# A long convolution and two expert layers: PSUM laid out by stage, the imaginary product in a pair of banks, both folds on VectorE, and the first products at another pace

## The chip, the cores and the metric

The kernel runs on one core of a Trainium2 chip. The core has five engines that run side by side and wait for each other through semaphores: TensorE (PE: matmuls, and PEld: their weight loads), VectorE (DVE), ScalarE (ACT), GpSimd (POOL) and SyncE (SP), whose queue issues nearly all DMA transfers. SBUF is the working memory. PSUM is the small memory that matmuls write; here it is used as 8 banks of 512 fp32 words for each of 128 partitions. [...]

The metric is the device time of one execution in microseconds (us).

## The reference

```python
def _attn_ref(x, v, pos_emb, w1, w2):                    # S = 12480, D = 128
    h_filt = (np.maximum(pos_emb @ w1, 0.0) @ w2) * np.exp(-0.01 * np.arange(S))[:, None]
    u = x * v
    Uf = np.fft.rfft(u, n=2 * S, axis=1)
    Hf = np.fft.rfft(h_filt, n=2 * S, axis=0)
    y = np.fft.irfft(Uf * Hf[None, :, :], n=2 * S, axis=1)[:, :S, :]
    return x * y

def reference(...):
    x = attn_out                                         # 12480 tokens of 128 channels
    x = (np.maximum(x @ w_in, 0.0) ** 2) @ w_out         # 2048 hidden units
    h = x @ w_in2
    return (np.maximum(h, 0.0) + alpha * np.minimum(h, 0.0)) @ w_out2
```

## The kernel before

The convolution is computed in the frequency domain, on a grid of 110 x 229 points, with small dense transform matrices instead of an FFT. Its work is cut into these parts:

- The filter: `z_stage` and `ar_stage` compute the filter's values and their first transform; `r_stage` does the second in 28 steps of two frequencies and spills the result to DRAM, 14 pieces.
- The signal, in two halves of 64 channels: `u_stage(h)` has 16 groups of four channels (k = 16h to 16h + 15) and runs in 17 steps. A step holds `u_mm_a` of one group and `u_mm_b` of the group before. `u_mm_a` is 16 matmuls (line 267) into two banks, a ScalarE copy (270), and a sum and a difference on VectorE (272). `u_mm_b` transforms the difference (280, 281) and the sum (284): ScalarE copies the odd part to `t` (283), VectorE writes even + t and even - t into U (287). A step also loads a later group's inputs (243) and multiplies x and v for the group three ahead on GpSimd (`prep`, line 251, two instructions).
- The product with the filter, `p_stage(h)`, 14 steps of four frequencies. A step loads a piece of the filter two steps ahead (322); for c = 0 (real) and c = 1 (imaginary) it makes the filter's values H with matmuls (329) and multiplies U by them on VectorE (334; in the first half U lies in two pieces, so this is two instructions). The products A and B lie in one tile T, two of which alternate. The complex product is then folded in place: A's even words minus B's odd ones on VectorE (341), A's odd words plus B's even ones on GpSimd (308). Last, the sum and the difference of neighbouring entries go back into U (314): in the first half four GpSimd instructions, in the second half two; in a half's last step the sums are VectorE's. Lines 308 and 314 of a step are issued one step later (`late`).
- The inverse transform, `b_stage(h)`, 16 groups of 16 matmuls (353), two banks a group, copied out by ScalarE (361). It needs all of U of its half, so it can't start before the last 314 of `p_stage(h)`. `y_stage` finishes the convolution.
- The expert layers, `moe`, fill the time from 489 us to the end; the weights are prepared for them beside `b_stage(1)` and `y_stage`.

The instructions of an engine run in the order in which the program issues them; no scheduler moves them. `run(...)` sets that order: each generator has a pace, and the one that lags most is advanced by a step. Three calls matter here: `u_stage(0)` with `r_stage`; then `u_stage(1)` (17 steps) with `p_stage(0)` at a pace of nj + 1 = 15 (nj is 14); then `p_stage(1)` with `b_stage(0)`.

The banks are shared out by rings: `r_a` (0, 1) for line 267, `r_b` (2 to 4) for 280 to 284, `r_h` (5 to 7) for `r_stage` and H, `r_ab` (0 to 4) for `b_stage(0)`.

Of the kernel before, what the change touches and what calls it, by code (L numbers as in the profile page):

```python
# [9 lines left out]
F32 = mybir.dt.float32  # L10
# [12 lines left out]
K2 = 2 * KA  # L23
HB = (NB + 1) // 2
# [7 lines left out]
DG = 4  # L32
NG = DH // DG
# [17 lines left out]
def ring_of(pool, n, shape, dtype, name):  # L51
    return Ring(pool.tile(shape, dtype, name=f"{name}{i}") for i in range(n))
# [3 lines left out]
def kernel(  # L56
# [21 lines left out]
    nc = tc.nc  # L78
    PSUM = bass.MemoryType.PSUM
# [2 lines left out]
    dram = ctx.enter_context(tc.tile_pool(name="dram", bufs=1, space=bass.MemoryType.DRAM))  # L82
    s_g = ExitStack()
    p_g = s_g.enter_context(tc.tile_pool(name="p_g", bufs=1, side="right"))
    psum = ctx.enter_context(tc.tile_pool(name="psum", bufs=1, space=PSUM))
    banks = [psum.tile([128, 512], F32, name=f"bank{i}") for i in range(8)]
    r_any, r_a, r_b, r_h = Ring(banks), Ring(banks[0:2]), Ring(banks[2:5]), Ring(banks[5:8])
    r_ab, r_y = Ring(banks[0:5]), Ring(banks[0:6])

    def bank(ring, p, *dims):  # L90
        n = 1
        for d in dims:
            n *= d
# [180 lines left out]
    def u_mm_b(k):  # L274
        h, g = divmod(k, NG)
        a = a_t.pop(k)
        po = bank(r_b, HB, DG, 2, KA)
        pe = bank(r_b, HB, DG, K2)
        ao = a[:, 1].rearrange("p d (k c) -> p d k c", c=2)
        nc.tensor.matmul(po[:, :, 0], lhsT=nsinb, rhs=ao[:, :, :, 1])  # L280
        nc.tensor.matmul(po[:, :, 1], lhsT=sinb, rhs=ao[:, :, :, 0])
        t = t_ring[k % 2][:HB]
        nc.scalar.copy(out=t.rearrange("p d (k c) -> p d k c", c=2), in_=po.rearrange("p d c k -> p d k c"))
        nc.tensor.matmul(pe, lhsT=cosb, rhs=a[:, 0])  # L284
        u = U(h, 2 * DG * g, 2 * DG).rearrange("p (d s) k -> p d s k", s=2)
        for s, op in ((0, ALU.add), (1, ALU.subtract)):
            nc.vector.tensor_tensor(out=u[:, :, s], in0=pe, in1=t, op=op)

    def u_stage(h):
        for k in range(h * NG, (h + 1) * NG + 1):  # L290
            if k < (h + 1) * NG:
                load(k + NX - 1)
                u_mm_a(k)
                prep(k + NX - 3)
            if k > h * NG:
                u_mm_b(k - 1)
            yield

    nj = KP // 2
# [1 line left out]
    p_order += [(j + nj - 6) % nj for j in range(nj)]  # L301

    def p_stage(h, t_ring, r_ring):
        late = []

        def finish(n, j, A, B):
            last = n % nj == nj - 1
            nc.gpsimd.tensor_tensor(out=A[:, :, :, 1], in0=A[:, :, :, 1], in1=B[:, :, :, 0], op=ALU.add)  # L308
            for x0, m in parts(h):
                y = A[:, x0:x0 + m].rearrange("p (d s) k c -> p d s (k c)", s=2)  # L310
                u = U(h, x0, m).rearrange("p (d s) k -> p d s k", s=2)[:, :, :, 8 * j:8 * j + 8]
                for s, op in ((0, ALU.add), (1, ALU.subtract)):
                    eng = nc.vector if last and s == 0 else nc.gpsimd
                    eng.tensor_tensor(out=u[:, :, s], in0=y[:, :, 0], in1=y[:, :, 1], op=op)  # L314

        for n in range(h * nj, (h + 1) * nj):
            j = p_order[n]
            m = p_order[min(n + 2, 2 * nj - 1)]
            if m not in r_t:
                del r_t[p_order[n - 1]]  # L320
                r_t[m] = r_ring()
                nc.sync.dma_start(out=r_t[m].rearrange("p q c k -> p (q c k)"), in_=spill[m])
            r = r_t[j]
            T = t_ring()
            for c in range(2):
                H = bank(r_h, HB, DH, 2, 2, 2)
                for q in range(2):
                    for s in range(2):
                        nc.tensor.matmul(  # L329
                            H[:, :, s, q], lhsT=r[:, q, 2 * s + c], rhs=w2_sb[:, h * D:(h + 1) * D]  # L330
                        )
                hv = H.rearrange("p d s q r -> p (d s) (q r)")
                for x0, m in parts(h):
                    nc.vector.tensor_tensor(
                        out=T[:, c, x0:x0 + m],
                        in0=U(h, x0, m)[:, :, 8 * j:8 * j + 8].rearrange("p x (k c) -> p x k c", c=2),
                        in1=hv[:, x0:x0 + m].unsqueeze(3).to_broadcast([HB, m, 4, 2]),
                        op=ALU.mult,
                    )
            A, B = T[:, 0], T[:, 1]  # L340
            nc.vector.tensor_tensor(out=A[:, :, :, 0], in0=A[:, :, :, 0], in1=B[:, :, :, 1], op=ALU.subtract)
            if late:
                late.pop()()
            late.append(lambda n=n, j=j, A=A, B=B: finish(n, j, A, B))
            yield
        late.pop()()

    def b_stage(h, alone):
        for g in range(NG):
# [183 lines left out]
    n = NCH * NT  # L533
# [141 lines left out]
    with tc.manual_schedule():  # L675
        with ExitStack() as st:
            late = st.enter_context(tc.tile_pool(name="late", bufs=1))
            w2_sb = late.tile([128, 2 * D], F32, name="w2_sb")
            dfa = late.tile([NA, K2], F32, name="dfa")
            dfa_f = late.tile([NA, K2], F32, name="dfa_f")  # L680
            r_ring = ring_of(late, 3, [128, 2, 4, HB], F32, "r")
            with tc.tile_pool(name="early", bufs=1) as early:
                run((z_stage(*load_first(early)), 1))
                run((ar_stage(early), 1))
            with tc.tile_pool(name="rt", bufs=1) as rt:
                run((u_stage(0), NG + 1), (r_stage(rt, r_ring), KP))
            big = st.enter_context(tc.tile_pool(name="tt", bufs=1))
            tt = ring_of(big, 2, [HB, 2, D, 4, 2], F32, "T")
            p0, q0 = p_stage(0, tt, r_ring), p_stage(1, tt, r_ring)
            run((u_stage(1), NG + 1), (p0, nj + 1))  # L690
            run((q0, nj + 3), (b_stage(0, False), NG))
        wa = ctx.enter_context(tc.tile_pool(name="wa", bufs=1))
        wst = ctx.enter_context(tc.tile_pool(name="wst", bufs=1))
        decode = weights(wst)
# [179 lines left out]
```

## Time and profile before

| | |
|---|---|
| median of 3 runs | 1478.89 us (1477.95 to 1481.53) |
| the profiled execution | 1478.57 us; span of the profile 1476.8 us |
| busy over the span | PE 1441.3 us, DVE 1174.6, ACT 966.9, POOL 1042.9 |
[...]
| chain that ended last | PE 89%, POOL 5%, DVE 3%, issue 2%, DMA 1% |
| `u_stage(0)` with `r_stage` | from about 60 to 138 us |
| `u_stage(1)` with `p_stage(0)` | 138.6 to 235.8 us |
| `p_stage(1)` with `b_stage(0)` | 235.8 to 299.5 us |
| `b_stage(1)`, first matmul | 299.48 us |

The profile is one execution, and times in it count from the start of its span. Busy time of an engine is the time in which an instruction of it runs; waits are not in it, except where an instruction is held up after its start. The lines named are those of the kernel before. A row of the timeline may stand for several instructions in a row ("x4"); its duration then covers them all.

### The profile page before, as it was taken

The page shows a single profiled execution, that of the slowest core. Times are in us where ns is not written, and L with a number is a line of the kernel's source. Part 1 is how long each engine was busy: PE and PEld are TensorE (multiplying, and loading weights), DVE is VectorE, ACT ScalarE, POOL GpSimd, SP SyncE. Part 2 cuts the span into 40 slices and gives each one's busy share as a digit, 9 for nine tenths or more (in the row PEclk, how much of TensorE's full clock was granted, in tenths as well). Part 3 has the DMA queues.
Part 4 walks back from the last instruction along what each step waited for, and adds up shares of the span by engine and source line. Part 5 has one row for each costly group of instructions (what it writes and reads, how often), then busy time and mean ns, then how long its engine had stood idle before and what let it go on. Part 6 is the DMA issues. An engine that isn't in the chain of part 4 may idle for free.

```text
span 1476.8 us, 23093 instructions
## 1 busy us (share of the span) xinstructions
PE 1441.3 (98%) x7634; PEld 1231.4 (83%) x7634; DVE 1174.6 (80%) x1852; ACT 966.9 (65%) x1857; POOL 1042.9 (71%) x851
## 2 busy tenths in 40 slices
PE   8999888889999999999999999999999999999998
PEld 8989778789888888888888888888888888888887
DVE  5978998769778877777777777777777787777998
ACT  5333112262588777777777777777777777777776
POOL 2245998944677777777777777777777777777766
PEclk9999989999999999999999999999999999999999
DMA  9388922239600000000000000000000000000000
GB/s 285 94 217 230 211 84 78 65 106 278 205 22 8 1 8 8 1 8 8 8 8 8 7 2 8 7 8 8 8 1 8 8 8 8 8 8 1 15 15 14
DMA packets 73869, 76.83 MB, mean 52 GB/s; under 512 B 6739, under 2 KB 65428, under 8 KB 73364
## 3 DMA queue, kind: packets, MB, share of 16 engines
q1 hardware_dynamic: 72650, 71.12, 17.4%
q0 software_dynamic: 688, 3.93, 0.8%
q8 instruction: 60, 0.98, 0.3%
q14 instruction: 62, 0.50, 0.1%
q10 hardware_dynamic: 409, 0.29, 0.1%
HBM read 58.41 MB, written 16.92 MB: 51 GB/s over the span
## 4 chain that ended last, share of the span: by engine, by line
PE 89%; POOL 5%; DVE 3%; issue 2%; DMA 1%; ACT 0%; POOLq 0%; DVEq 0%; ACTq 0%
PE bank L565 24%; PE bank L566 24%; PE bank L567 24%; PE bank L267 3%; PE bank L353 2%; PE bank L168 2%; PE bank L407 2%; PE bank L406 2%; DVE R L205 2%; PE bank L223 2%; POOL R L314 2%; POOL T L308 2%; PE bank L284 1%; PE bank L329 1%; PE bank L280 1%
## 5 line engine op out<-in xcount | busy, mean ns | idle before, releaser
L618 POOL TENSOR_TENSOR g<-R,g 128x500 fp32r<-128x500 f32 (+1 forms) x598 | 776.9, 1320 | 279.6 <-ACT g L607 204.2
L600 DVE SCALAR_TENSOR_TENSOR R<-bank,e 128x500 f32<-128x500 f32 (+1 forms) x800 | 531.4, 674 | 172.3 <-POOL g L618 95.4
L607 ACT CAST g<-R 128x500 fp32r<-128x500 f32 (+1 forms) x800 | 466.3, 604 | 32.3 <-DVE R L600 28.4
L585 ACT ACTIVATE e<-bank 128x500 f32<-128x500 f32 (+1 forms) x400 | 234.7, 587 | 165.2 <-PE bank L567 162.1
L590 DVE TENSOR_SCALAR e<-bank,alpha 128x500 f32<-128x500 f32 (+1 forms) x266 | 195.3, 734 | 50.4 <-PE bank L567 50.1
L618 DVE TENSOR_TENSOR g<-R,g 128x500 fp32r<-128x500 f32 (+1 forms) x202 | 158.2, 784 | 0.0
L566 PE MATMUL bank<-g,w_o 128*128 128x500 f32 (+1 forms) x400 | 155.7, 389 | 0.4 <-POOL g L618 0.4
L567 PE MATMUL bank<-g,w_o 128*128 128x500 f32 (+1 forms) x400 | 155.5, 389 | 0.0
L566 PE MATMUL bank<-x,w_i 128*128 128x500 f32 (+1 forms) x400 | 155.4, 388 | 0.0
L565 PE MATMUL bank<-x,w_i 128*128 128x500 f32 (+1 forms) x400 | 155.2, 388 | 0.0
L565 PE MATMUL bank<-g,w_o 128*128 128x500 f32 (+1 forms) x400 | 155.0, 388 | 0.0
L567 PE MATMUL bank<-x,w_i 128*128 128x500 f32 (+1 forms) x400 | 155.0, 387 | 0.0
L567 PE MATMUL bank<-g,w_o0b 128*128 128x500 f32 (+1 forms) x350 | 136.4, 390 | 0.0
L566 PE MATMUL bank<-g,w_o0b 128*128 128x500 f32 (+1 forms) x350 | 136.3, 389 | 0.0
L565 PE MATMUL bank<-g,w_o0b 128*128 128x500 f32 (+1 forms) x350 | 135.7, 388 | 0.0
L251 POOL TENSOR_TENSOR G<-G 110x460 f32<-110x460 f32 x64 | 73.9, 1174 | 86.7 <-DMA G<-in_vs_dram 49.3
L587 ACT ACTIVATE e<-bank 128x500 f32<-128x500 f32 (+1 forms) x134 | 78.8, 588 | 39.3 <-PE bank L567 38.6
L588 ACT ACTIVATE e<-e,alpha 128x500 f32<-128x500 f32 (+1 forms) x134 | 95.6, 714 | 4.4
L566 PEld LDWEIGHTS bank<-x,w_i 128*128 128x128 f32 x400 | 75.1, 188 | 15.9
L566 PEld LDWEIGHTS bank<-g,w_o 128*128 128x128 f32 x400 | 75.2, 188 | 15.8 <-POOL g L618 0.8
L565 PEld LDWEIGHTS bank<-x,w_i 128*128 128x128 f32 x400 | 75.3, 188 | 15.6
L565 PEld LDWEIGHTS bank<-g,w_o 128*128 128x128 f32 x400 | 75.2, 188 | 15.4
(107 smaller groups left out, 2632.1 us busy)
## 6 DMA issues: line engine op xcount, KB each, us to landing
G<-in_vs_dram SPq DMA_DIRECT2D x64, 224.0 KB, 5.5
r<-spill SPq DMA_DIRECT2D x22, 460.0 KB, 4.2
G<-in_xs_dram SPq DMA_DIRECT2D x32, 224.0 KB, 5.4
spill<-r SPq DMA_DIRECT2D x14, 460.0 KB, 3.0
out_dram<-R SPq DMA_DIRECT2D x24, 250.0 KB, 2.0
R<-in_xt_dram SPq DMA_DIRECT2D x27, 218.0 KB, 3.8
s_w<-in_moe_w_in_dram SPq DMA_DIRECT2D x16, 256.0 KB, 3.4
s_w<-in_moe_w_out_dram SPq DMA_DIRECT2D x16, 256.0 KB, 3.6
```

Of the source, the lines that this page charges most:

```text
L251: nc.gpsimd.tensor_tensor(out=u[:, :, 0:HB], in0=u[:, :, 0:HB], in1=y, op=ALU.mult)
L267: nc.tensor.matmul(p[s][:, d], lhsT=u[s][:, d], rhs=dfa)
L565: nc.tensor.matmul(p, lhsT=wl, rhs=xh, start=first, stop=False)
L566: nc.tensor.matmul(p, lhsT=wh, rhs=xl, start=False, stop=False)
L567: nc.tensor.matmul(p, lhsT=wh, rhs=xh, start=False, stop=last)
L585: nc.scalar.activation(out=r, in_=p, func=ACTF.Relu)
L587: nc.scalar.activation(out=r, in_=p, func=ACTF.Relu, scale=-1.0)
L588: nc.scalar.activation(out=r, in_=r, func=ACTF.Copy, scale=alpha[:, t:t + 1])
L590: nc.vector.tensor_scalar(out=r, in0=p, scalar1=0.0, scalar2=alpha[:, t:t + 1], op0=ALU.min, op1=ALU.mult)
L600: nc.vector.scalar_tensor_tensor(out=g, in0=p, scalar=0.0, in1=r, op0=ALU.max, op1=op)
L607: nc.scalar.copy(out=gh, in_=g)
L618: eng.tensor_tensor(out=gl, in0=g, in1=gh.bitcast(F32), op=ALU.subtract)
```

## The change

1. PSUM is laid out anew for two stages. After `u_stage(0)` the pool of eight banks is closed and another opened, with six banks and one tile of two banks, `wide`. `r_a`, `r_b` and `r_h` have two banks each, `r_ab` four. Before `b_stage(1)` the eight banks come back.
2. The imaginary product B is written to `wide`, not to SBUF. T holds A alone.
3. Both folds are VectorE's; the GpSimd sum (308) is gone. The finishing instructions (314) are issued at the end of their own step, all on GpSimd, but for the very last step, whose two are VectorE's.
4. In `u_mm_b` the matmul of the even part goes first. In the second half ScalarE also copies the even part to one of two tiles, `even`, and GpSimd computes even - t from it; VectorE keeps even + t.
5. `p_stage(0)` runs at a pace of nj - 2 = 12 instead of 15.

```diff
-    psum = ctx.enter_context(tc.tile_pool(name="psum", bufs=1, space=PSUM))
-    banks = [psum.tile([128, 512], F32, name=f"bank{i}") for i in range(8)]
+    s_psum = ctx.enter_context(ExitStack())
+
+    def lay_banks(name, n):
+        s_psum.close()
+        pool = s_psum.enter_context(tc.tile_pool(name=name, bufs=1, space=PSUM))
+        tiles = [pool.tile([128, 512], F32, name=f"{name}{i}") for i in range(n)]
+        if n < 8:
+            tiles.append(pool.tile([128, (8 - n) * 512], F32, name=f"{name}_wide"))
+        return tiles
...
     def u_mm_b(k):
         h, g = divmod(k, NG)
         a = a_t.pop(k)
+        pe = bank(r_b, HB, DG, K2)
         po = bank(r_b, HB, DG, 2, KA)
-        pe = bank(r_b, HB, DG, K2)
+        nc.tensor.matmul(pe, lhsT=cosb, rhs=a[:, 0])
+        even = None
+        if h:
+            even = even_ring[0]()
+            nc.scalar.copy(out=even, in_=pe)
         ao = a[:, 1].rearrange("p d (k c) -> p d k c", c=2)
...
-        nc.tensor.matmul(pe, lhsT=cosb, rhs=a[:, 0])
         u = U(h, 2 * DG * g, 2 * DG).rearrange("p (d s) k -> p d s k", s=2)
-        for s, op in ((0, ALU.add), (1, ALU.subtract)):
-            nc.vector.tensor_tensor(out=u[:, :, s], in0=pe, in1=t, op=op)
+        nc.vector.tensor_tensor(out=u[:, :, 0], in0=pe, in1=t, op=ALU.add)
+        if h:
+            nc.gpsimd.tensor_tensor(out=u[:, :, 1], in0=even, in1=t, op=ALU.subtract)
+        else:
+            nc.vector.tensor_tensor(out=u[:, :, 1], in0=pe, in1=t, op=ALU.subtract)
...
-        def finish(n, j, A, B):
-            last = n % nj == nj - 1
-            nc.gpsimd.tensor_tensor(out=A[:, :, :, 1], in0=A[:, :, :, 1], in1=B[:, :, :, 0], op=ALU.add)
+        def finish(n, j, A):
+            eng = nc.vector if n == 2 * nj - 1 else nc.gpsimd
...
-            T = t_ring()
-            for c in range(2):
+            A = t_ring()
+            B = wide[:HB].rearrange("p (x k c) -> p x k c", k=4, c=2)
+            for c, out_c in enumerate((A, B)):
...
-            A, B = T[:, 0], T[:, 1]
-            nc.vector.tensor_tensor(out=A[:, :, :, 0], in0=A[:, :, :, 0], in1=B[:, :, :, 1], op=ALU.subtract)
-            if late:
-                late.pop()()
-            late.append(lambda n=n, j=j, A=A, B=B: finish(n, j, A, B))
+            for c, op in ((0, ALU.subtract), (1, ALU.add)):
+                nc.vector.tensor_tensor(out=A[:, :, :, c], in0=A[:, :, :, c], in1=B[:, :, :, 1 - c], op=op)
+            finish(n, j, A)
             yield
-        late.pop()()
...
+            *few, wide = lay_banks("pb", 6)
+            r_a.items, r_b.items, r_h.items, r_ab.items = few[0:2], few[2:4], few[4:6], few[0:4]
             big = st.enter_context(tc.tile_pool(name="tt", bufs=1))
-            tt = ring_of(big, 2, [HB, 2, D, 4, 2], F32, "T")
+            tt = ring_of(big, 2, [HB, D, 4, 2], F32, "T")
+            even_ring.append(ring_of(big, 2, [HB, DG, K2], F32, "even"))
             p0, q0 = p_stage(0, tt, r_ring), p_stage(1, tt, r_ring)
-            run((u_stage(1), NG + 1), (p0, nj + 1))
+            run((u_stage(1), NG + 1), (p0, nj - 2))
             run((q0, nj + 3), (b_stage(0, False), NG))
+        banks = lay_banks("bank", 8)
+        r_y.items = banks[0:6]
```

GpSimd, late in `u_stage(1)` with `p_stage(0)`, from the last input products on, before (T_1102 and T_1103 are the two tiles T; 314 finishes a step, 251 is the pair of input products, 308 the imaginary sum):

```order
L314 TENSOR_TENSOR G<-T_1103 115x56x8 x2
L251 TENSOR_TENSOR G<-G 110x4x115 x2
L308 TENSOR_TENSOR T_1102<-T_1102 115x512
L314 TENSOR_TENSOR G<-T_1102 115x8x8 x2
L314 TENSOR_TENSOR G<-T_1102 115x56x8 x2
L308 TENSOR_TENSOR T_1103<-T_1103 115x512
L314 TENSOR_TENSOR G<-T_1103 115x8x8 x2
L314 TENSOR_TENSOR G<-T_1103 115x56x8 x2
```

And the same place now (lines of the changed kernel: 327 finishes, 260 is the pair of input products, 302 the subtract that moved here; T_1113, T_1114 and even_1115, even_1116 are the tiles of the two rings):

```order
L327 TENSOR_TENSOR G<-T_1113 115x8x8 x2
L327 TENSOR_TENSOR G<-T_1113 115x56x8 x2
L260 TENSOR_TENSOR G<-G 110x4x115 x2
L302 TENSOR_TENSOR R_78<-even_1116,G 115x4x112
L327 TENSOR_TENSOR G<-T_1114 115x8x8 x2
L327 TENSOR_TENSOR G<-T_1114 115x56x8 x2
L302 TENSOR_TENSOR R_78<-even_1115,G 115x4x112
L302 TENSOR_TENSOR R_78<-even_1116,G 115x4x112
```

The sum 308 ahead of each finishing group is gone, and one or two subtracts of the transform stand between two finishing groups.

VectorE, at the passage from the first half's products to the second half's, before (272 and 287 belong to `u_stage(1)`, 334 is the product, 341 the fold, 314 the finishing sums of the half's last step):

```order
L341 TENSOR_TENSOR T_1103<-T_1103 115x512
L272 TENSOR_TENSOR G<-G,bank_70 115x4x112 x2
L287 TENSOR_TENSOR R_78<-bank_72,G 115x4x112 x2
L314 TENSOR_TENSOR G<-T_1103 115x8x8
L314 TENSOR_TENSOR G<-T_1103 115x56x8
L287 TENSOR_TENSOR R_78<-bank_71,G 115x4x112 x2
L334 TENSOR_TENSOR T_1102<-R_78,bank_76 115x1024
L334 TENSOR_TENSOR T_1102<-R_78,bank_74 115x1024
L341 TENSOR_TENSOR T_1102<-T_1102 115x512
```

And now (348 is the product, 355 the two folds, pb_1107 and pb_1108 the two banks of H, pb_wide the pair of banks for B):

```order
L355 TENSOR_TENSOR T_1113<-T_1113,pb_wide 115x512 x2
L348 TENSOR_TENSOR T_1114<-G,pb_1107 115x128
L348 TENSOR_TENSOR T_1114<-G,pb_1107 115x896
L348 TENSOR_TENSOR pb_wide<-G,pb_1108 115x128
L348 TENSOR_TENSOR pb_wide<-G,pb_1108 115x896
L355 TENSOR_TENSOR T_1114<-T_1114,pb_wide 115x512 x2
L348 TENSOR_TENSOR T_1113<-R_78,pb_1107 115x1024
L348 TENSOR_TENSOR pb_wide<-R_78,pb_1108 115x1024
L355 TENSOR_TENSOR T_1113<-T_1113,pb_wide 115x512 x2
L348 TENSOR_TENSOR T_1114<-R_78,pb_1107 115x1024
```

The last steps of the first half now follow each other with no work of the transform between them, the finishing sums have left VectorE, and each step has two folds that read `pb_wide`.

## Rows read from the trace of the kernel before

**Rows 1.** The two stages: busy time (instructions) by engine, granted clock, DMA share, GB/s.

```profile
138.60:235.80 97.20, 85.34 (x576) 73.88 (x575) 94.52 (x136) 16.50 (x31) 89.25 (x90) 0.91 0.58 137
235.80:299.50 63.70, 50.93 (x467) 48.79 (x466) 46.48 (x44) 17.46 (x32) 60.01 (x41) 1.00 0.27 83
```

**Rows 2.** Instructions of line 341 in stage 1: ns min/median/max.

```profile
L341 DVE TENSOR_TENSOR T<-T x14: 692/2432/2467, 142.2 to 230.6; 115x512 f32<-115x512 f32 x14
```

**Rows 3.** Groups by line in stage 1: busy us, mean ns | idle before, releasers.

```profile
L314 POOL TENSOR_TENSOR G<-T 115x448 f32<-115x448 f32 x27 | 30.0, 1131 | 0.0
...
L308 POOL TENSOR_TENSOR T<-T 115x512 f32<-115x512 f32 x14 | 27.2, 1940 | 8.3 <-DVE T L334 8.3
L251 POOL TENSOR_TENSOR G<-G 110x460 f32<-110x460 f32 x22 | 25.6, 1188 | 0.0
...
L283 ACT COPY G<-bank 115x448 f32<-115x448 f32 x16 | 8.5, 532 | 37.2 <-PE bank L281 32.6 <-DVE T L334 4.6
L270 ACT COPY G<-bank 115x448 f32<-115x448 f32 x16 | 8.5, 532 | 42.6 <-PE bank L267 37.0 <-DVE G L272 5.6
```

**Rows 4.** Groups by line in stage 2.

```profile
L314 POOL TENSOR_TENSOR R<-T 115x512 f32<-115x512 f32 x27 | 39.9, 1501 | 1.1
L334 DVE TENSOR_TENSOR T<-R,bank 115x1024 f32<-115x1024 f32 x28 | 32.9, 1218 | 14.0 <-POOL R L314 13.9
...
L308 POOL TENSOR_TENSOR T<-T 115x512 f32<-115x512 f32 x14 | 21.5, 1538 | 4.2 <-DVE T L334 4.2
```

**Rows 5.** Timeline of one step of stage 1: start us, duration us, what.

```profile
202.56 1.15 DVE L287 TENSOR_TENSOR R<-bank,G 115x448 f32<-115x448 f32 x2
203.02 2.77 POOL L314 TENSOR_TENSOR G<-T 115x64 f32<-115x64 f32 x4
...
203.62 2.47 DVE L334 TENSOR_TENSOR T<-G,bank 115x128 f32<-115x128 f32 x4
203.70 1.77 PE L267 MATMUL bank<-dfa,G 110*115 110x112 f32 x16
...
205.31 0.57 PE L280 MATMUL bank<-G,dfb 115*115 115x224 f32 x2
...
205.75 2.29 POOL L251 TENSOR_TENSOR G<-G 110x460 f32<-110x460 f32 x2
...
206.86 1.91 PE L329 MATMUL bank<-w_sb,r 128*115 128x128 f32 x16
```

**Rows 6.** Timeline, VectorE's line 205 in the filter's transform.

```profile
54.29 8.45 DVE L205 TENSOR_TENSOR R<-ar_p,bank 115x448 f32<-115x448 f32 x10 [0.37 <-issue]
```

**Rows 7.** Groups by line on VectorE, 300 to 490 us.

```profile
L452 DVE TENSOR_TENSOR bank<-bank,w_o 128x256 f32<-128x256 f32 x7 | 3.0, 423 | 0.0
```

**Rows 8.** Timeline of stage 2: its start, one step, its end.

```profile
235.84 1.75 PE L353 MATMUL bank<-dfb,G 115*112 115x116 f32 x16
...
283.76 2.35 DVE L334 TENSOR_TENSOR T<-R,bank 115x1024 f32<-115x1024 f32 x2 [1.17 <-POOL R L314]
...
298.64 0.69 DVE L314 TENSOR_TENSOR R<-T 115x512 f32<-115x512 f32 x1 [2.59 <-POOL T L308]
...
299.48 28.64 PE L353 MATMUL bank<-dfb,R 115*112 115x116 f32 x256 [4.08 <-DVE R L314]
```

**Rows 9.** Timeline from the first half to stage 1.

```profile
136.73 1.77 PE L267 MATMUL bank<-dfa,G 110*115 110x112 f32 x16
...
137.67 0.39 DVE L230 TENSOR_TENSOR r<-bank,rt 128x230 f32<-128x230 f32 x1
...
139.67 2.47 DVE L334 TENSOR_TENSOR T<-G,bank 115x128 f32<-115x128 f32 x4
```

**Rows 10.** Three stretches of 10 us, columns as in rows 1.

```profile
120.00:130.00 10.00, 10.00 (x80) 9.05 (x80) 7.45 (x18) 3.61 (x9) 5.89 (x6) 1.00 1.09 292
140.00:150.00 10.00, 10.00 (x80) 9.03 (x79) 9.93 (x14) 2.13 (x4) 7.63 (x8) 1.00 1.11 251
180.00:190.00 10.00, 8.13 (x45) 6.73 (x44) 9.93 (x14) 1.60 (x3) 9.92 (x10) 0.83 0.71 182
```

More of the change, by code (lines that the diff above doesn't have):

```diff
@@ L84 @@
     p_g = s_g.enter_context(tc.tile_pool(name="p_g", bufs=1, side="right"))
-    psum = ctx.enter_context(tc.tile_pool(name="psum", bufs=1, space=PSUM))
-    banks = [psum.tile([128, 512], F32, name=f"bank{i}") for i in range(8)]
+    s_psum = ctx.enter_context(ExitStack())
[7 more added lines that the diff above has]
+    banks = lay_banks("bank", 8)
     r_any, r_a, r_b, r_h = Ring(banks), Ring(banks[0:2]), Ring(banks[2:5]), Ring(banks[5:8])
-    r_ab, r_y = Ring(banks[0:5]), Ring(banks[0:6])
+    r_ab, r_y = Ring([]), Ring([])
     def bank(ring, p, *dims):
@@ L260 @@
     a_t = {}
+    even_ring = []
     def u_mm_a(k):
@@ L303, in p_stage @@
     def p_stage(h, t_ring, r_ring):
-        late = []
-        def finish(n, j, A, B):
-            last = n % nj == nj - 1
-            nc.gpsimd.tensor_tensor(out=A[:, :, :, 1], in0=A[:, :, :, 1], in1=B[:, :, :, 0], op=ALU.add)
+        def finish(n, j, A):
+            eng = nc.vector if n == 2 * nj - 1 else nc.gpsimd
             for x0, m in parts(h):
@@ L312, in finish @@
                 for s, op in ((0, ALU.add), (1, ALU.subtract)):
-                    eng = nc.vector if last and s == 0 else nc.gpsimd
                     eng.tensor_tensor(out=u[:, :, s], in0=y[:, :, 0], in1=y[:, :, 1], op=op)
@@ L334, in p_stage @@
                     nc.vector.tensor_tensor(
-                        out=T[:, c, x0:x0 + m],
+                        out=out_c[:, x0:x0 + m],
                         in0=U(h, x0, m)[:, :, 8 * j:8 * j + 8].rearrange("p x (k c) -> p x k c", c=2),
@@ L686 @@
                 run((u_stage(0), NG + 1), (r_stage(rt, r_ring), KP))
+            *few, wide = lay_banks("pb", 6)
+            r_a.items, r_b.items, r_h.items, r_ab.items = few[0:2], few[2:4], few[4:6], few[0:4]
             big = st.enter_context(tc.tile_pool(name="tt", bufs=1))
-            tt = ring_of(big, 2, [HB, 2, D, 4, 2], F32, "T")
+            tt = ring_of(big, 2, [HB, D, 4, 2], F32, "T")
+            even_ring.append(ring_of(big, 2, [HB, DG, K2], F32, "even"))
             p0, q0 = p_stage(0, tt, r_ring), p_stage(1, tt, r_ring)
-            run((u_stage(1), NG + 1), (p0, nj + 1))
+            run((u_stage(1), NG + 1), (p0, nj - 2))
             run((q0, nj + 3), (b_stage(0, False), NG))
+        banks = lay_banks("bank", 8)
+        r_y.items = banks[0:6]
         wa = ctx.enter_context(tc.tile_pool(name="wa", bufs=1))
```

## The prediction

> **What bounds the kernel now.** I read the page's chain of waits first, then a table of two stretches, then the instructions of each by line, then single steps in the timeline. The chain is the matmuls of the two expert layers for most of the span, which the change does not touch. Its pieces on GpSimd and VectorE all lie between 138 and 300 us, in the two stages that the change rewrites. I call them stage 1 (the second half's forward transform beside the first half's products, 138.6 to 235.8) and stage 2 (the second half's products beside the first half's inverse transform, 235.8 to 299.5). In stage 1 GpSimd is busy 89.25 of 97.2 us and VectorE 94.52; in stage 2 GpSimd 60.01 of 63.7, VectorE 46.48 [rows 1].
>
> VectorE's 94.52 is not all work. Its real-part fold L341 is the only instruction there with two SBUF inputs; alone it takes 692 ns, with GpSimd at work mostly 2.43 us [rows 2]. In stage 1 GpSimd hardly idles, and L308, the imaginary sum, costs it 1.94 us a step [rows 3]. In stage 2 GpSimd is the bound: L308 21.5 us and L314 39.9 us fill 61.4 of 63.7, and VectorE's product waits 13.9 us for L314 [rows 4]. PE stands behind both. So a microsecond taken from GpSimd in either stage comes off the end, until VectorE is next.
>
> **Units.** From one step of stage 1 [rows 5]: F, the four finishing instructions, 2.78 us; P, the pair of input products, 2.29; the four product instructions 2.47; a VectorE pair on 448 elements runs 1.15, next start after 1.06; PE takes 1.61 for 16 matmuls L267, 1.55 for L280 to L284, about 1.75 for 16 of L329 (1.91 with the last one's tail).
>
> **The folds.** L308 leaves GpSimd (14 x 1.94 us in stage 1, 14 x 1.54 in stage 2 [rows 3, 4]) and becomes a second VectorE fold. Both folds now read B from PSUM, so no VectorE instruction of these stages has two SBUF inputs, and the 2.43 us of L341 should fall to its undisturbed price. Low bound 0.69 us for 512 elements [rows 2]; the second of a pair adds 0.54 x 512/448 = 0.61; a pair costs 1.30. High bound: L205, a strided VectorE operation with a PSUM input, needs 8.45/10 = 0.845 us for 448 elements [rows 6], that is 0.97 for 512 and about 2.05 for the pair. I take 1.30. The new folds read every second word as L341 does, and ScalarE's L283, which reads PSUM words 224 bytes apart, takes the 532 ns of the contiguous L270 [rows 3]: the step in PSUM alone costs nothing there. [...] The products written to PSUM I price as before: L452, with PSUM output, takes 423 ns for 256 elements [rows 7], about what length alone explains.
>
> So a step on VectorE costs D = 2.47 + 1.30 = 3.77 in stage 1 and 2.35 [rows 8] + 0.05 + 1.30 = 3.70 in stage 2.
>
> **The subtract moved in the forward transform.** VectorE loses 16 instructions of 0.6 us in stage 1; GpSimd gains 16 on 448 elements, C. Bounds: 1.13 us, the mean of L314 on as many, and 1.19, that of L251 on 460 [rows 3]; I take 1.13. ScalarE gains 16 copies of 0.53 us; it is busy 16.5 of 97 us [rows 1], so they hide. But they add a wait. The "even" ring has two slots, and GpSimd now also reads t, so ScalarE's copies for a group wait until GpSimd has done C two groups earlier. Behind them on ScalarE stands the next group's copy, and VectorE's sum waits for t.
>
> **Order and entry.** F of a step comes right behind its folds, no longer a step late; the first F stands ahead of one P that was done before it, so 12 P follow it instead of 11. The new banks lie in the space of the closed pool, so the first matmul waits for that pool's last reader: L230 ends at 138.06, where L267 started at 136.73 [rows 9]. I take 1.4 us (low bound 0). In the first half PE is busy 10.00 of 10 us from 120 to 130 [rows 10]; the even product swapped ahead of the odd one hides behind it and costs 0 (if each of 15 groups showed 0.7 us, 11 us). Products now go 14 to 17 transform steps at 12 to 17 in pace, so the last two run after the transform. On SP's queue the spill reads come later between the input loads. From 140 to 150 the DMA engines are full [rows 10], yet GpSimd waited for none in stage 1; loads are issued two transform steps ahead: 0, up to 3 us.
>
> **Sum for stage 1.** The first product started at 139.67 [rows 9]; now 141.07, its folds end at 144.84, and F can start. GpSimd then has 14 F + 12 P + 16 C = 38.9 + 27.5 + 18.1 = 84.5 us, and would end at 229.3. VectorE has 14 x 3.77 + 15 x 1.06 + 16 x 0.58 = 78: less, but badly spread. Up to the twelfth transform step GpSimd does 9 F, 12 P, 12 C = 66.1, to 210.9. P is then over, and VectorE must do the rest: the last of these C frees the slots for two ScalarE copies (1.15), then the sum (0.58), the eleventh product step, a transform step (1.65), the twelfth, a last sum (0.58), the thirteenth and fourteenth, and F. That is 210.9 + 1.15 + 0.58 + 4 x 3.77 + 1.65 + 0.58 + 2.78 = 232.7. The inverse transform's first matmul L353 needs that last F; it started at 235.84 [rows 8]. Gain 3.1 us.
>
> **Sum for stage 2.** VectorE does its first step meanwhile. The second waits for PE: 16 matmuls of L353 (1.75 [rows 8]) and eight of L329 (0.87): 235.3. Then 13 steps x 3.70 = 48.1, to 283.4; GpSimd's F, at most 3.0 us [rows 4], is under the step, and PE's 16 + 16 matmuls, about 3.4, too. The last finishing pair is VectorE's own, 1.3, against L308, a wait and 0.69 [rows 8]; PE picks up 0.15 later: 284.9. L353 started at 299.48 [rows 8]. Gain 14.6 in all. What follows starts from this point and is unchanged.
>
> The profiled execution took 1478.57 us (span 1476.8), 0.3 under the median of 1478.89. 1478.57 - 14.6 = 1464.0.
>
> **Rival 1, folds at L205's rate: 1478.** The chain after 210.9, which the first folds shift to 211.7, becomes 211.7 + 1.15 + 0.58 + 4 x 4.52 + 1.65 + 0.58 + 2.78 = 236.5; stage 2 is 236.5 + 2.6 + 13 x 4.45 + 1.45 = 298.4, 1.1 us before 299.48. [...] Against: L283 and L341 at full rate. 0.20.
>
> **Rival 2, the tail's wait is hidden: 1461.** If the copies for the last groups find their slots free, stage 1 ends with GpSimd's 229.3 and the gain is 18.0. For it: nothing but the roughness of 0.1 us a piece in a chain of twelve. Against: the ring has two slots, and GpSimd is the later engine. 0.06.
>
> [...]
>
> A fold dearer than any VectorE row (over 1.25 us) would be slower too: 0.05.
>
> **Chances and range.** Forecast 0.65, rivals 0.20, 0.06, 0.04, dear folds 0.05. A measurement here can tell 0.3%, 4.4 us, so faster ends at 1474.5. Of rival 1, folds between the bounds included, a third ends under that. Faster 0.65 + 0.06 + 0.07 = 0.78; same 0.12; slower 0.10. The forecast's own range is 1460 to 1469 (1.4 us of entry, 3 of DMA, a fold pair within 0.2); it reaches down to 1459 for rival 2 and up to 1479 for rival 1.
>
> **What will show it.** Right: no GpSimd imaginary sum; folds near 0.69 us each; stage 2 steps of 3.7 us with VectorE nearly always busy and GpSimd idle a fifth; the inverse transform starting near 233 and the second one near 285; VectorE's late sums in stage 1 waiting for ScalarE, and that for GpSimd. Wrong: folds near 1.05 us (rival 1); GpSimd ending stage 1 without a gap (rival 2); a granted clock under 0.75 in stage 1 (rival 3); idle GpSimd waiting for input loads.

## The result, and the profile after

The kernel after takes 1458.89 us, the median of four runs (1456.75 to 1462.23), against 1478.42 us for the kernel before beside it. The ratio is 0.9869 with a 95% interval of 0.9857 to 0.9881: 1.3% faster. Forecast were 1464.0 us and a range of 1459 to 1479, so the time lies just under the range's low end.

The profiled execution took 1459.62 us (span 1457.8 us), 18.95 less than the one before, where 14.6 were forecast. Where they came from is read from the first matmul of each later stage. Each column is one execution: in the profiles of e8 and e12 below, which run the code of the kernel before up to `b_stage(1)`, `b_stage(0)` starts at 236.66 and 238.46, so that a start is known to about 2.6 us only.

| first matmul of | before, us | after, us | gained so far |
|---|---|---|---|
| `b_stage(0)` (stage 2) | 235.84 | 231.97 | 3.87 (forecast 3.1) |
| `b_stage(1)` | 299.48 | 283.51 | 15.97 (forecast 14.6) |
| `y_stage` | 327.98 | 309.81 | 18.17 (forecast 14.6) |
| end (profiled executions) | 1478.57 | 1459.62 | 18.95 (forecast 14.6) |

The two stages, with the columns of [rows 1]: length, then busy time (instructions) of PE, PEld, DVE, ACT and POOL, granted clock, DMA share, GB/s.

```profile
140.70:232.00 91.30, 81.07 (x585) 70.93 (x584) 79.97 (x133) 25.15 (x48) 80.58 (x94) 0.97 0.61 142
232.00:283.50 51.50, 50.83 (x464) 48.78 (x465) 50.61 (x58) 17.46 (x32) 34.72 (x29) 1.00 0.34 102
```

In stage 2 GpSimd falls from 60.01 to 34.72 us and stops being the bound; VectorE (50.61 of 51.5) now fills the stage, and PE (50.83) shows next to no idle time either. In stage 1 no engine is full over the whole stretch.

The groups by line of stage 1, VectorE and GpSimd, answer to [rows 2, 3]. The numbers behind the bar are the idle time ahead of the group and what ended it.

```profile
L282 DVE TENSOR_TENSOR G<-G,pb 115x448 f32<-115x448 f32 x32 | 18.3, 614 | 6.6 <-PE pb L277 6.6
L355 DVE TENSOR_TENSOR T<-T,pb_wide 115x512 f32<-115x512 f32 x28 | 18.0, 685 | 0.5
L348 DVE TENSOR_TENSOR pb_wide<-G,pb 115x896 f32<-115x896 f32 x14 | 15.3, 1096 | 0.5
L348 DVE TENSOR_TENSOR T<-G,pb 115x896 f32<-115x896 f32 x14 | 15.1, 1079 | 0.0
L300 DVE TENSOR_TENSOR R<-pb,G 115x448 f32<-115x448 f32 x16 | 9.9, 619 | 5.6 <-ACT G L298 5.5
...
L302 POOL TENSOR_TENSOR R<-even,G 115x448 f32<-115x448 f32 x16 | 18.1, 1132 | 0.0
L327 POOL TENSOR_TENSOR G<-T 115x64 f32<-115x64 f32 x28 | 8.3, 313 | 19.1 <-DVE T L355 19.1
```

The folds (355) cost 685 ns each, with GpSimd at work or not: over both stages their minimum, median and maximum are 679, 687 and 692 ns, where [rows 2] had 692, 2432 and 2467. By the trace 37 of the 56 began while a GpSimd instruction was running, and 19 beside an idle GpSimd; both kinds lie between 679 and 692 ns. Writing a product to PSUM (`pb_wide`) costs 17 ns more than writing it to SBUF (1096 against 1079).

The groups of stage 2, which answer to [rows 4]:

```profile
L327 POOL TENSOR_TENSOR R<-T 115x512 f32<-115x512 f32 x26 | 32.4, 1265 | 14.0 <-DVE T L355 14.0
...
L348 DVE TENSOR_TENSOR pb_wide<-R,pb 115x1024 f32<-115x1024 f32 x14 | 17.1, 1223 | 0.0
L348 DVE TENSOR_TENSOR T<-R,pb 115x1024 f32<-115x1024 f32 x14 | 17.0, 1214 | 0.0
```

The wait has turned round. Before, VectorE's product waited 13.9 us for GpSimd's finishing; now GpSimd's finishing (327) waits 14.0 us for VectorE's folds, and VectorE's products wait for nothing.

### The profile page after: what moved, and what is told of

It reads as the page before. It is cut to its first block, busy times and chain, and to the rows that moved or that the text cites. A ratio compares the mean times of both kernels' runs of the same rounds, so it can differ in the third digit from the quotient of the medians.

```text
span 1457.8 us, 23121 instructions
## 1 busy us (share of the span) xinstructions
PE 1434.3 (98%) x7634; PEld 1226.4 (84%) x7634; DVE 1157.9 (79%) x1863; ACT 974.2 (67%) x1873; POOL 1005.4 (69%) x840
## 4 chain that ended last, share of the span: by engine, by line
PE 87%; DVE 5%; POOL 3%; issue 2%; ACT 1%; DMA 1%; SPq 0%; POOLq 0%; DVEq 0%; ACTq 0%
PE bank L576 25%; PE bank L577 24%; PE bank L578 24%; PE bank L177 2%; PE bank L418 2%; PE bank L417 2%; DVE R L214 2%; PE bank L232 2%; PE bank L277 2%; DVE pb_wide L348 1%; PE pb L343 1%; DVE T L355 1%; POOL G L327 1%; PE bank L289 1%; POOL G L260 1%
## 5 line engine op out<-in xcount | busy, mean ns | idle before, releaser
L629 DVE TENSOR_TENSOR g<-R,g 128x500 fp32r<-128x500 f32 (+1 forms) x202 | 154.4, 765 | 0.0
```

The costliest lines, as they stand in the source:

```text
L629: eng.tensor_tensor(out=gl, in0=g, in1=gh.bitcast(F32), op=ALU.subtract)
```

## The experiments

Eight kernels start from the kernel after, two from the kernel before. Lines of code in a row are those of the kernel it is from. Times are medians; each ratio is to the kernel before, timed on the same chip.

### Is it the place of B? (e1b)

```diff
-            A = t_ring()
-            B = wide[:HB].rearrange("p (x k c) -> p x k c", k=4, c=2)
+            T = t_ring()
+            A, B = T[:, 0], T[:, 1]
...
-            tt = ring_of(big, 2, [HB, D, 4, 2], F32, "T")
+            tt = ring_of(big, 2, [HB, 2, D, 4, 2], F32, "T")
```

Not shown: the small table `dfa_f` moves to a pool that closes earlier, to make room. A first form without that move (e1) asked for 19.5 KB of each partition for T, where 19.41 were left, so it has no time; 1475 to 1490 us had been expected of it.

> The kernel after, with the imaginary product B in SBUF beside A instead of in the pair of PSUM banks; both folds stay on VectorE, all else is unchanged but for the place of one small table. Theory (a fold with two SBUF inputs is held up while GpSimd works, 2.43 us against 0.69 in the rows of before, and one input from PSUM frees it): the folds' mean rises from 0.69 to 1.4 to 2.4 us; VectorE's step in stage 2 rises from 3.59 by 1.0 to 2.5 us (at most by GpSimd's 2.5 us a step), so 14 to 35 us there, and stage 1 by 10 to 45 us, since VectorE's busy sum of 80 takes 28 folds more dearly: time 1480 to 1540, slower than both kernels. Rival (where B lies doesn't matter, the gain comes from taking the sum off GpSimd): folds near 0.7 us, time 1457 to 1462.

Measured: 1476.46 us, ratio 0.9985 [0.9976, 0.9995], some 17 us more than the kernel after and outside both ranges above, though inside that given for e1. Its two stages, and its folds in each:

```profile
140.70:246.70 106.00, 86.48 (x579) 74.49 (x577) 91.86 (x133) 25.01 (x47) 83.53 (x94) 0.91 0.51 122
246.70:300.00 53.30, 52.69 (x465) 49.94 (x464) 52.74 (x58) 17.45 (x32) 34.78 (x29) 0.99 0.32 99
```

```profile
L355 DVE TENSOR_TENSOR T<-T x28: 680/1102/1690, 144.5 to 245.5; 115x512 f32<-115x512 f32 x28
L355 DVE TENSOR_TENSOR T<-T x28: 678/750/1090, 248.5 to 298.0; 115x512 f32<-115x512 f32 x28
```

Stage 1 becomes 14.7 us longer (the inverse transform starts at 246.7 instead of 231.97), stage 2 only 1.8. In stage 1 the folds take 31.3 us instead of 18.0, 13.3 us more and most of the difference. In stage 2 the same folds with two SBUF inputs run nearly undisturbed (the first of a pair mostly near 825 ns, the second 680), because GpSimd waits for just these folds (16.0 us in all) and so stands still for most of their time.

The trace also shows what a fold with two SBUF inputs waits for. Of the 56 folds of e1b, 26 began beside an idle GpSimd and took 678 to 695 ns. The other 30 began while a GpSimd instruction was running, and each ended 0.55 us after such an instruction. The 28 folds of the kernel before do the same (6 of 692 to 694 ns; 22 that end 0.55 us after a GpSimd instruction). One pair of e1b:

```profile
192.75 3.18 DVE L355 TENSOR_TENSOR T<-T 115x512 f32<-115x512 f32 x2
...
191.55 2.29 POOL L260 TENSOR_TENSOR G<-G 110x460 f32<-110x460 f32 x2
193.80 1.58 POOL L302 TENSOR_TENSOR R<-even,G 115x448 f32<-115x448 f32 x1
```

The first fold ends at 194.38, 0.54 us after the second input product (193.84); the second ends at 195.93, 0.55 us after the subtract (195.38), which itself took 1.58 us instead of 1.13. So the price of such a fold is here what is left of the GpSimd instruction beside it, plus 0.55 us. In the kernel before a fold often waited out two input products, hence its 2.43 us; in e1b mostly the end of one instruction, hence less than the 1.4 to 2.4 us that I expected.

So in stage 1 the change rests on PSUM, and in stage 2 hardly: there the gain seems to be that the sum left GpSimd, the bound of that stage before. No run puts the sum alone back.

### Is it the subtract on GpSimd? (e4)

```diff
-        if h:
-            even = even_ring[0]()
-            nc.scalar.copy(out=even, in_=pe)
...
-        if h:
-            nc.gpsimd.tensor_tensor(out=u[:, :, 1], in0=even, in1=t, op=ALU.subtract)
-        else:
-            nc.vector.tensor_tensor(out=u[:, :, 1], in0=pe, in1=t, op=ALU.subtract)
+        nc.vector.tensor_tensor(out=u[:, :, 1], in0=pe, in1=t, op=ALU.subtract)
```

> The changed kernel with the subtract even - t of the second half back on VectorE, without ScalarE's even copies. Theory: GpSimd's stage-1 sum falls by 16 x 1.13 = 18 us to 66, VectorE's rises by 16 x 0.55 = 9 us to 87, so VectorE is the bound of the whole stage; the stage takes about 87 us from the first product, as now: within 3 us of the changed kernel, 1456 to 1462 us. Rival (the move of the subtract is a main source of the gain): 8 us or more slower, 1467 and above.

Measured: 1467.96 us, ratio 0.9927 [0.9911, 0.9944]; my theory fell, and the rival's 1467 and above holds. The inverse transform starts at 239.88, 7.9 us later than in the kernel after. Stage 1 of this kernel, and three groups of it (348 is the fold here, 320 the finishing, 296 the sum even + t, 294 the copy to `t`):

```profile
138.00:240.00 102.00, 88.31 (x593) 76.59 (x594) 89.62 (x152) 17.05 (x32) 64.01 (x79) 0.92 0.56 131
```

```profile
L296 DVE TENSOR_TENSOR R<-pb,G 115x448 f32<-115x448 f32 x16 | 9.9, 619 | 8.1 <-ACT G L294 8.1
...
L277 PE MATMUL pb<-dfa,G 110*115 110x112 f32 x256 | 30.1, 268 | 10.8 <-POOL G L320 8.7 <-DVE r L239 1.7 <-DVE G L282 0.5
...
L320 POOL TENSOR_TENSOR G<-T 115x64 f32<-115x64 f32 (+1 forms) x55 | 37.7, 719 | 44.1 <-DVE T L348 44.1
```

VectorE's 16 subtracts of 0.61 us (9.8 us) are back, and the stage is 7.9 us longer although VectorE idles 8.1 us in it. Reading the waits backwards: GpSimd's finishing instructions wait 44.1 us for folds (14.3 of them at the entry); the next input products stand behind them on GpSimd, so PE waits 8.7 us for these, ScalarE for PE and VectorE for ScalarE. With VectorE this full, GpSimd does not run ahead, and its waits come back to VectorE. This chain is read from the waits; the time is measured.

### Does the pace matter? (e3)

```diff
-            run((u_stage(1), NG + 1), (p0, nj - 2))
+            run((u_stage(1), NG + 1), (p0, nj + 1))
```

> The changed kernel with the first half's products at the old pace, nj + 1 = 15 instead of nj - 2 = 12. Theory (stage 1 is bound by GpSimd until its input products are over, and then by VectorE, to which the slow pace leaves too many steps): with the old pace the last steps are fewer, VectorE's tail is shorter and the inverse transform starts 2 to 4 us earlier: 1455 to 1458 us. Rival (the wider spread is a source of the gain): 3 us or more slower, 1462 and above.

Measured: 1458.16 us, ratio 0.9862 [0.9847, 0.9877]; `b_stage(0)` starts at 231.56, 0.4 us earlier. In this kernel the pace gives and takes nothing that can be measured. The time lies just above the theory's 1455 to 1458, but the 2 to 4 us that it had forecast are not there, and the rival's loss is not either.

### The entry: one layout all along (e5), two banks kept (e9), products earlier (e6)

After the change of layout PE stands idle, because the new banks wait for the last reader of the old ones, and what follows is late. Timeline of the kernel after: start us, duration us, what.

```profile
139.08 3.09 PE L277 MATMUL pb<-dfa,G 110*115 110x112 f32 x16 [1.74 <-DVE r L239]
...
143.48 1.28 DVE L348 TENSOR_TENSOR T<-G,pb 115x128 f32<-115x128 f32 x2
...
147.56 2.78 POOL L327 TENSOR_TENSOR G<-T 115x64 f32<-115x64 f32 x4 [15.26 <-DVE T L355]
```

PE's 16 matmuls take 3.09 us here and 1.77 before the change [rows 9]; the granted clock between 140 and 150 us is 0.86, where it was 1.00 [rows 10]. The first product comes 3.8 us later than before, forecast was 1.4. The first matmul starts 2.35 us later, 0.45 of which PE was behind before its wait (its last matmuls of `r_stage` started at 136.30 against 135.85); the other 1.5 us arise between that matmul and the first product, where the granted clock was 0.68 (138 to 142 us).

e5 uses the later layout from the start, so that no pool is closed; `wide`'s halves serve as third banks of the rings:

```diff
-    banks = lay_banks("bank", 8)
-    r_any, r_a, r_b, r_h = Ring(banks), Ring(banks[0:2]), Ring(banks[2:5]), Ring(banks[5:8])
+    *few, wide = lay_banks("pb", 6)
+    banks = few + [wide[:, 0:512], wide[:, 512:1024]]
+    r_any, r_a = Ring(banks), Ring(banks[0:2])
+    r_b, r_h = Ring(banks[2:4] + banks[6:7]), Ring(banks[4:6] + banks[7:8])
```

> The changed kernel with one PSUM layout for the whole program: six banks and the wide tile from the start, its two halves serving as the third bank of two rings in the first half and as banks 6 and 7 later; no pool is closed. Theory (the new pool makes the first matmul of stage 1 wait for the last reader of the old one; PE idles 1.7 us and then works at the lower clock): the first product of stage 1 starts 2 to 4 us earlier and the whole is that much faster, 1455 to 1457 us. Rival (the entry is hidden, since stage 1 is bound by GpSimd, which has slack before its first finishing group): no change, 1458 to 1460.

Measured: 1510.11 us, ratio 1.0218 [1.0201, 1.0235], the worst of all. PE has lost time long before the entry; between 30 and 60 us:

```profile
30.00:60.00 30.00, 23.18 (x180) 22.63 (x181) 16.48 (x20) 9.17 (x30) 9.29 (x9) 0.89 0.26 61
```

The kernel after has 28.72 us busy there at a clock of 1.00. The inverse transform starts 20 us late (251.8), and some 30 us more go after the inverse transforms, 18.4 of them as waits of PE ahead of the expert layers' matmuls into `pb_wide`. PE's waits in the first 60 us name matmuls into `pb_wide` that wait for VectorE and ScalarE (8.1 us in all). That the two halves of one tile are waited for as one is my reading; no run takes it apart. The question of the entry was drowned by it.

e9 keeps two banks (those of the first matmuls) in a pool that is never closed; e6 leaves the layout alone and lets GpSimd make the input products one group earlier, inside its idle 15.26 us; e10 has both; e11 has both and the old pace:

```diff
+    keep = ctx.enter_context(tc.tile_pool(name="keep", bufs=1, space=PSUM))
+    kept = [keep.tile([128, 512], F32, name=f"keep{i}") for i in range(2)]
...
-        tiles = [pool.tile([128, 512], F32, name=f"{name}{i}") for i in range(n)]
+        tiles = kept + [pool.tile([128, 512], F32, name=f"{name}{i}") for i in range(n - 2)]
```

```diff
-                prep(k + NX - 3)
+                prep(k + NX - 3 + h)
```

> The kernel after, with GpSimd's pair of input products issued one unit earlier all through the second half, so that one pair (2.29 us by its row) falls into GpSimd's idle 15.26 us at the entry instead of into its busy chain. Theory (GpSimd's sum is what bounds stage 1): the first matmul of the inverse transform comes 2.0 to 2.3 us earlier (near 229.8) and the time is 1456.2 to 1457.2. Rival (VectorE's tail, with its folds and waits, decides the end of stage 1 as predicted): start of the inverse transform within 0.7 us of 231.97, time 1458.2 to 1459.6.

> The kernel after, with the first two PSUM banks (those of the u products' first matmuls) in a place of their own that is not closed at the change of layout, so that the first matmuls of stage 1 needn't wait for VectorE's last sums of the stage before. Theory (the entry's wait is part of the chain): the first matmul of stage 1 starts near 137.4 instead of 139.08, the first product on VectorE near 141.5 instead of 143.48, and the time falls by 1.5 to 2.5 us to 1456.4 to 1457.4. Rival (the entry's gap is made up before stage 1 ends, since GpSimd catches up or VectorE's tail decides): time within 0.5 us of 1458.9, start of the inverse transform within 0.7 us of 231.97.

> Both edits: two banks kept and GpSimd's input products one unit earlier. If both lengthen the same chain (GpSimd's), the gains add: start of the inverse transform near 228, time 1454.5 to 1455.5. If VectorE's tail takes over after the first of them, the second gives under 0.7 us: time 1456.3 to 1457.2. If neither chain matters, 1458.2 to 1459.6.

> Both edits of e10 (two banks kept, input products one unit earlier) and the steps of stage 1 at the old pace. In e10 GpSimd stood idle between 200 and 232 us (11.69 busy of 15.00 and 13.21 of 17.00) while VectorE worked through the last steps, so that those steps come too late for it. Theory (with GpSimd's slack the pace now matters; earlier steps shorten the tail): the inverse transform starts 1 to 3 us before e10's 229.6, time 1453.5 to 1455.5. Rival (VectorE's sum sets the end whatever the order, as e3 showed for the kernel after): time within 0.7 us of e10's 1456.3. Other rival (the folds now stand in VectorE's queue ahead of sums that GpSimd waits for): 1457 or more.

| kernel | median (lowest to highest), us | ratio to before | `b_stage(0)` starts, us |
|---|---|---|---|
| after | 1458.89 (1456.75 to 1462.23) | 0.9869 [0.9857, 0.9881] | 231.97 |
| e6, products earlier | 1457.63 (1456.68 to 1458.84) | 0.9857 [0.9844, 0.9870] | 231.7 |
| e9, two banks kept | 1458.05 (1457.78 to 1458.34) | 0.9860 [0.9845, 0.9875] | 230.3 |
| e10, both | 1456.31 (1455.91 to 1456.60) | 0.9847 [0.9834, 0.9861] | 229.6 |
| e11, both, old pace | 1455.10 (1454.92 to 1455.78) | 0.9842 [0.9828, 0.9855] | 228.48 |

e6 and e9 alone lie between their theories and rivals; in time neither can be told from the kernel after. The starts of `b_stage(0)` are of one execution each, and the spread of 2.6 us named above holds for them too: what follows on single edits is read from the traces and is not a measured gain. By the traces e9's entry works as meant, from its timeline:

```profile
137.51 1.77 PE L279 MATMUL keep<-dfa,G 110*115 110x112 f32 x16
...
140.45 1.28 DVE L350 TENSOR_TENSOR T<-G,pb 115x128 f32<-115x128 f32 x2
```

No wait ahead of the matmuls, 1.77 us again, and the first product 3.0 us earlier; 1.7 of these 3.0 are left where the inverse transform starts. e6's transform starts within 0.3 us of the kernel after, as its rival had it: GpSimd gets ahead (it waits 2.31 us for the first of the last four steps instead of 0.66), and VectorE, without a gap from 213.06 to the end of the stage, decides. Together they start 2.4 us earlier, 0.7 more than e9 alone; the time, 1456.31, is that of the second case of e10's expectation (VectorE's tail takes over). e11 lies inside its first theory (1453.5 to 1455.5, start 1 to 3 us earlier): 1.1 us earlier than e10 in the trace, 1.2 less in the medians. But the two ran on different chips, and their ratios differ by 0.0005 with intervals that overlap for the most part, so that the pace's share is not shown. e10's and e11's slowest runs are faster than the fastest of the kernel after; the interval of e10's ratio still overlaps with its own, that of e11's just does not. So the three edits together are shown to gain, and no single one is. e11 is the fastest of all, 23 us under the kernel before.

### The inverse transform's own speed (e8, e12)

What I had not forecast at all is that `b_stage(1)` runs faster in the kernel after. One row of its timeline, which answers to the last of [rows 8], and the stretches of that stage before and after:

```profile
283.51 25.91 PE L364 MATMUL bank<-dfb,R 115*112 115x116 f32 x256 [0.68 <-issue]
```

```profile
299.50:328.00 28.50, 28.50 (x257) 28.46 (x257) 17.43 (x41) 20.79 (x48) 12.62 (x17) 0.89 0.38 97
```

```profile
283.50:309.80 26.30, 25.86 (x256) 25.51 (x256) 17.48 (x42) 20.14 (x48) 11.66 (x16) 1.00 0.42 105
```

The same 256 matmuls take 25.91 us instead of 28.64; the granted clock is 1.00 instead of 0.89. Ahead of them PE was idle 4.08 us before, and now 0.68. In e8 and e12 the kernel before gets matmuls nobody uses in that gap, 19 and 15 of them:

```diff
             run((q0, nj + 3), (b_stage(0, False), NG))
+            fill = banks[0][:HB, 0:HX]
+            for _ in range(19):
+                nc.tensor.matmul(fill, lhsT=dfb[:, 0, :HB], rhs=icosb)
```

> The kernel before, with 19 matmuls that nobody uses put on TensorE between the end of the first inverse transform and the start of the second, over the 4.08 us in which it stood idle there. Theory (in the kernel after, the second inverse transform runs 2.2 us faster, 26.3 against 28.5 us, because TensorE no longer stands idle ahead of it): the start stays near 299.5 us, the run of 28.6 us falls to 26.2 to 26.8, the granted clock of 300:330 rises from 0.90 to 0.98 or more, and the time falls by 1.5 to 2.4 us, to 1476.0 to 1477.0. Rival (the idle time has nothing to do with it, or the fillers delay the start): 28.3 us or more, time 1478 to 1480.

> The kernel before with 15 unused matmuls in TensorE's idle 4.08 us instead of 19 (19 took 4.09 us and let the second inverse transform start at 300.2 instead of 299.5). Theory: TensorE's run of 256 matmuls again takes 26.2 to 26.8 us instead of 28.6, the start is back within 0.4 us of 299.5, what follows it starts 1.2 to 2.2 us earlier than the 327.98 of before, time 1476.5 to 1477.9. Rival (a short gap left ahead of the run is enough to slow it, or the start drifts as it did): run of 28 us or more, or the time within 0.7 us of before.

Groups of PE in `b_stage(1)`, for before, e8 and e12 in this order (the stretch read ends at 328 us, ahead of e12's last four matmuls):

```profile
L353 PE MATMUL bank<-dfb,R 115*112 115x116 f32 x256 | 28.6, 280 | 4.1 <-DVE R L314 4.1
```

```profile
L353 PE MATMUL bank<-dfb,R 115*112 115x116 f32 x256 | 26.3, 264 | 0.4 <-ACT G L361 0.3
```

```profile
L353 PE MATMUL bank<-dfb,R 115*112 115x116 f32 x252 | 25.9, 264 | 1.5 <-DVE R L314 0.9 <-ACT G L361 0.6
```

The theory's mechanism is shown twice: with the gap filled a matmul takes 264 ns instead of 280, the granted clock is 1.00 (e8, 300.2 to 327.3 us), and e8's run is 2.3 us shorter. In e12 a gap of 0.87 us was left ahead of the run, and its matmuls take 264 ns all the same.

In time the gain is not clear of noise: 1478.01 us (ratio 0.9996 [0.9987, 1.0005]) and 1477.89 (0.9995 [0.9986, 1.0004]), no difference from before. The traces say where to look. e8's run began at 300.22 and e12's at 301.65, later than the 299.48 of before, but so had stage 2 in these executions (236.66 and 238.46 against 235.84), ahead of the first filler: the fillers didn't delay it. Counted from the start of stage 2, what follows the run starts after 92.14 us in the kernel before, 90.64 in e8 (at 327.30) and 90.59 in e12 (at 329.05): 1.5 us less in both. These are three executions; the intervals of the times, down to 0.9987 and 0.9986 (some 2 us), allow such a gain and don't show it.

e1b bears on the same question. Its `b_stage(1)` starts at 300.08, 0.6 us later than in the kernel before, behind a gap of 0.68 us; its matmuls take 263 ns, `y_stage` starts at 325.93, 2.05 us earlier than before, and its time is 0.15% under that of the kernel before, by an interval that leaves out 1. So all of its small gain lies behind the start of that run.

## Why the prediction was right, and where it was off

**The folds were priced right, for a reason that held in stage 1 alone.** Forecast 0.69 us each, found 0.685; rival 1 (folds at L205's rate) is out, since every one of 56 folds took at most 692 ns. A fold that reads every second fp32 word of PSUM took 679 to 692 ns, as one with two SBUF inputs beside an idle GpSimd does (678 to 695 in e1b). I put the low price down to B's place in both stages. e1b shows that in stage 2 GpSimd's idleness would have given most of it: 1.8 of the stage's 12.1 us hang on PSUM, against 14.7 us in stage 1. (The fold was not quite the only VectorE instruction with two SBUF inputs, as I wrote: the finishing sums of a half's last step have two as well.)

**Stage 1: forecast 3.1 us, found 3.87, by errors that cancel.** The wait I named stands in the trace (start us, duration us, what):

```profile
212.37 0.53 ACT L293 COPY even<-pb 115x448 f32<-115x448 f32 x1 [3.42 <-POOL R L302]
...
213.37 0.62 DVE L300 TENSOR_TENSOR R<-pb,G 115x448 f32<-115x448 f32 x1 [1.50 <-ACT G L298]
```

A copy waits for GpSimd, the sum for the copy, and from 213.37 to the last folds VectorE works without a gap. Over the stage ScalarE waits 13.3 us for GpSimd in this way. The copy at 212.37 is the one that the sum had starting at 210.9: GpSimd had done the 9 F, 12 P and 12 C by then, and from the end of the twelfth subtract (212.3) to the end of the last finishing group it took 22.1 us, forecast 21.8. But the entry cost 3.8 us instead of 1.4, by a later start of PE and a low clock behind its wait, and the first finishing group started 2.7 us late (147.56 against 144.84). GpSimd's chain made up 1.4 us of that, and the last finishing group ended at 234.37, not 232.7. And the inverse transform didn't wait for the end of it: its first matmul needs only the small pieces, which a finishing group does first:

```profile
231.60 2.77 POOL L327 TENSOR_TENSOR G<-T 115x64 f32<-115x64 f32 x4 [1.09 <-DVE T L355]
231.97 1.66 PEld L364 LDWEIGHTS pb<-dfb,G 115*112 115x112 f32 x16 [0.79 <-POOL G L327]
```

That step of the sum ("needs that last F") was wrong by the 2.4 us between 231.97 and 234.37, and hid the entry's size. It was no reading of the kernel before either: there the last finishing sums end at 234.80, and PE comes to 353 at 235.84 from 16 matmuls of 329 without a wait. With single executions that differ by up to 2.6 us at this point, a miss of only 0.8 us is in part luck.

**Stage 2: forecast 11.5 us, found 12.1.** VectorE's second step started at 235.03 (forecast 235.3), but not for the reason given: it did not wait for PE, it followed the first step (231.44) without a gap. A step took 3.59 us (forecast 3.70). Steps of the kernel after in the timeline:

```profile
263.75 1.22 DVE L348 TENSOR_TENSOR T<-R,pb 115x1024 f32<-115x1024 f32 x1
263.92 2.49 POOL L327 TENSOR_TENSOR R<-T 115x512 f32<-115x512 f32 x2 [1.10 <-DVE T L355]
...
264.88 1.22 DVE L348 TENSOR_TENSOR pb_wide<-R,pb 115x1024 f32<-115x1024 f32 x1
...
266.14 1.29 DVE L355 TENSOR_TENSOR T<-T,pb_wide 115x512 f32<-115x512 f32 x2
...
267.35 1.22 DVE L348 TENSOR_TENSOR T<-R,pb 115x1024 f32<-115x1024 f32 x1
```

From 263.75 to 267.35 is a step of 3.6 us. The pair of folds occupies VectorE 1.21 us until the next product starts (266.14 to 267.35), where I had put its whole duration, 1.30; over 13 steps that is 1.2 of the 1.4 us by which the stage ended earlier than 284.9. GpSimd was idle a third of the stage, not a fifth, since its pair of finishing instructions took 2.49 us and not up to 3.0. How much a still faster VectorE would gain here no run shows: PE's busy time (50.83 of 51.5 us) proves no bound, since e1b has 52.69 of 53.3 for the same matmuls; by my 3.4 us of PE a step it would be at most 0.2 us a step.

**"What follows is unchanged" was wrong by 2.2 us.** This is the largest error of the sum: 14.6 + 1.4 (start of `b_stage(1)`) + 2.2 (its run) + 0.8 (the rest) = 19.0. The row stood before me: a run of 28.64 us behind an idle of 4.08 us [rows 8]. I counted the idle time and did not ask what it did to the run. e8 and e12 show that filling the gap brings the mean matmul there from 280 to 264 ns. The range's low end, 1459, stood for rival 2 alone and held no term for this; 2.2 us more would put the median at 1461.1, inside the forecast's own range. The last 0.8 us, behind `y_stage`'s start, are not explained; the runs of one kernel differ by more.

**The other rivals.** Rival 2 (the tail's wait is hidden, 1461) had the nearer time, but its mechanism isn't in the trace: GpSimd doesn't end stage 1 without a gap, it waits 0.53 to 1.58 us ahead of each of its last four finishing groups. Rival 3 (a kernel slower by PE's clock in stage 1, chance 0.04) is out: no run shows a granted clock under 0.75 over that stage; it was 0.97 in the kernel after, 0.92 in e4 and 0.91 in e1b. The subtract's move, one term among others in my sum, is worth about 9 us by e4 (7.9 of them ahead of the inverse transform): without it the inverse transform would start 4 us later than in the kernel before, not 3.9 us earlier.

## What to carry to other kernels

When work moves off an engine, ask of each stretch what the other engine is doing when the instruction starts: the same operand's move to PSUM was worth 14.7 us where 16 of the 28 folds of e1b began beside a running GpSimd instruction and waited out what was left of it, and 1.8 us where GpSimd waited for the folds and only the first of a pair met what was left of one, mostly 0.3 us. An idle gap ahead of a run of matmuls can cost more than its length, here some 2 us behind a gap of 4.08: look at the clock of what follows, and forecast the gap's end as a term of its own. Edits that can't be told from nothing alone can show together (e11), so they are tried together; which of them gives what is then another question, and single executions don't answer it at this size.

## What the runs showed of the hardware that was not expected

- A VectorE fold with one SBUF and one PSUM input, every second word of each, took 679 to 692 ns for 512 elements whatever GpSimd did; with two SBUF inputs 678 to 1690 ns in e1b and up to 2467 in the kernel before. All 52 such folds of e1b and the kernel before that began beside a running GpSimd instruction ended 0.55 us (547 to 556 ns) after the end of one; the 32 others took 678 to 695 ns.
- GpSimd pays as well: its finishing instruction in stage 2 fell from 1501 to 1265 ns with the same work (1270 in e1b, where it waits for the folds instead of running beside them), its subtract in stage 1 from 1307 (e1b) to 1132 ns.
- After 4.08 us of idleness PE ran the next 28.5 us at a mean granted clock of 0.89, at 280 ns a matmul; without the gap at 1.00 and 263 or 264 ns. Gaps of 0.68 us (after, e1b), 0.7 us (e6) and 0.87 us (e12) ahead of the run left it at 263 or 264. After the 1.74 us at the entry, the clock of 140 to 150 us was 0.86.
